# The last gate's last 128 weight rows in three transfers on GpSimd's queue, ahead of everything else there

## The chip, the cores and the metric

One core of one Trainium2 chip runs the whole program. The metric is the time of one execution in microseconds on the device; lower is better. All inputs begin in HBM, and the output goes back there.

## The reference

One decode step of a transformer block for four sequences, with six modulation vectors from a conditioning vector `c`. All is fp32.

```
mod = silu(c) @ w_mod          # [4, 6*512]: sa, ca, ga, sb, cb, gb
h = layernorm(x) * (1 + ca) + sa
x = x + ga * attention(h)      # 32 query heads, 8 kv heads, the last 2048 positions
h = layernorm(x) * (1 + cb) + sb
x = x + gb * ((silu(h @ w1) * (h @ w3)) @ w2)     # 512 -> 1792 -> 512
```

The change concerns `gb`, the gate of the last line: gb = silu(c) @ (columns 2560 to 3071 of `w_mod`), a sum over 512 weight rows of 512 columns. These rows are taken in four chunks of 128.

## The kernel before

The program is written without a scheduler: each engine's instructions are in source order, and semaphores tie the engines together. Almost all loads are issued on SP's queue by the helper `load` (L89), in the order in which they are used. Each load has 128 partitions, and its semaphore counts 16 when it has landed.

Two SBUF buffers of 16384 columns, `KV[0]` and `KV[1]`, take the keys and values of the eight kv heads in turn; a third one, `WP`, takes the query and output projection weights. First of all comes `T0` (L91), which lies in `KV[1]`: 16 columns of `c`, transposed, and the weights of `ca` and `sa`. ACT's queue loads the first query weights (L92) and `x` (L93). `KV[0]` follows on SP, and `KV[1]` once the product with `T0` is done (`pe` 1, L95).

At the start DVE and ACT take the first layer norm's statistics from `x`, then silu of the 16 columns (L182 to L188) gives `sc`, the stationary operand of all modulation products. DVE's `same` (L179) stands between them and waits for `ident`, which POOL makes. POOL begins with memsets and `ident` (L128 to L139); after that it only passes on load semaphores.

Attention runs in a loop of four pairs of heads on PE and ACT. After it come the modulation products of the middle (L381), the second layer norm, and the FFN: `w1` and part of `w3` from `KV[0]`, the rest of `w3` (`f2_in`) from `KV[1]`. All of the last loads go into `KV[1]` in this order: `f2_in` in two halves, `gb_in` (the four chunks of the gate's weights, 2048 columns), and `w2` in six blocks (`W2_CUTS`, semaphores `dw`). On PE the gate's four products (L454) go to four groups of partitions in one PSUM bank, `bM`; they are summed later by a product with `same` (L474), which is also the transposition that the output needs. The FFN's down projection takes the first eight blocks of 128 rows into `bO`, the last six straight into `bX`. Two DVE steps (L488, L490) and a store (L492) end the program.

Of the kernel before, what the change touches and what calls it, by code (L numbers as in the profile page):

```python
# [5 lines left out]
AF = mybir.ActivationFunctionType  # L6
# [4 lines left out]
B, D, HQ, G, SK, DH, W, FF = 4, 512, 32, 8, 8192, 128, 2048, 1792  # L11
P = 128
# [2 lines left out]
EPS = 1e-5  # L15
CHUNKS = [(j, c) for c in range(4) for j in range(4) if c < 2 or j < 3]
HEAD = 8
W2_CUTS = [0, 4, 8, 10, 12, 13, 14]
PAIRS = G // 2

# [20 lines left out]
        return (self.sem, self.n)  # L41


def block_kernel(nc, x_in, t0_in, t1_in, kv_in, w_in, wm_in, f1_in, f2_in, gb_in, w2_in, out):
    T, v, s, gp, S = nc.tensor, nc.vector, nc.scalar, nc.gpsimd, nc.sync

    def sems(names):
        return [nc.alloc_semaphore(n) for n in names.split()]

    def sb(name, cols, rows=P):  # L50
        return nc.alloc_sbuf_tensor(name, (rows, cols), F32).ap()

    def bank(name):
        return nc.alloc_psum_tensor(name, (P, 512), F32).ap()

    (first,) = sems("first")
    A = Queue(nc, s, "act")
    V = Queue(nc, v, "dve")
    L = Queue(nc, gp, "pool")
    dx, dt0, dt1, dkv, dk, dva, dvb, dwo, dm, df1, df2a, df2b, dgb = sems("dx dt0 dt1 dkv dk dva dvb dwo dm df1 df2a df2b dgb")  # L60
    dw = sems(" ".join(f"dw{i}" for i in range(len(W2_CUTS) - 1)))
    z_ok, q_ok, p_ok, k_ok, va_ok, vb_ok, pt_ok, o_ok, ot_ok = sems("z_ok q_ok p_ok k_ok va_ok vb_ok pt_ok o_ok ot_ok")
    s_done, q_done, qt_done, pp_done, o_done, x_done, a_done, pe, last = sems("s_done q_done qt_done pp_done o_done x_done a_done pe last")
    (nm_ok, lb_ok, dout) = sems("nm_ok lb_ok dout")

    KV = [sb("KV0", 16384), sb("KV1", 16384)]
    WP = sb("WP", 8192)
    T0 = KV[1][:, : 16 + 4096]
    x_sb = sb("x_sb", 512, B)
    ident, same, eps = sb("ident", P), sb("same", B), sb("eps", 1)  # L70
    sc, e1, e2 = sb("sc", 16), sb("e1", 16), sb("e2", 16)
    hT, h2T = sb("hT", 16), sb("h2T", 16)
    Z = sb("Z", B * 28)
    q_sb, p_sb, o_sb, a_sb, y_sb, g_sb, u_sb, gb_sb = [sb(n, 512) for n in "q_sb p_sb o_sb a_sb y_sb g_sb u_sb gb_sb".split()]
# [10 lines left out]
    bS, bQ, bT, bP, bO, bX, bA, bM = [bank(n) for n in "bS bQ bT bP bO bX bA bM".split()]  # L85


    def load(dst, src, sem):
        S.dma_start(dst, src).then_inc(sem, 16)  # L89

    load(T0, t0_in, dt0)  # L91
    s.dma_start(WP[:, 4096:], t1_in).then_inc(dt1, 16)  # L92
# [27 lines left out]
    S.wait_ge(x_done, G)  # L120
    load(KV[1][:, :3072], f2_in[:, :3072], df2a)
    load(KV[1][:, 3072:6144], f2_in[:, 3072:], df2b)
    load(KV[1][:, 6144:8192], gb_in, dgb)
    for a, b, sem in zip(W2_CUTS[:-1], W2_CUTS[1:], dw):
        load(KV[1][:, 8192 + a * 512 : 8192 + b * 512], w2_in[:, a * 512 : b * 512], sem)


    l_eps = L.op(gp.memset(eps, EPS))  # L128
    t = L.op(gp.memset(ident, 0.0))
    L.wait(t)  # L130
# [48 lines left out]
    v_same = V.op(v.tensor_reduce(same, ident.rearrange("p (j i) -> p i j", i=32)[:, :B, :], axis=AX.X, op=ALU.add))  # L179

    A.wait((dt0, 16))
    t = A.op(s.activation(e1, T0[:, :16], AF.Exp, scale=-1.0))  # L182
    V.wait(t)
    t = V.op(v.tensor_scalar(e2, e1, 1.0, None, op0=ALU.add))
    V.wait(t)
    t = V.op(v.reciprocal(e2, e2))
    V.wait(t, (dt0, 16))
    t_sc = V.op(v.tensor_mul(sc, T0[:, :16], e2))  # L188

    A.wait((pe, 1))  # L190
    t_sa = A.op(s.copy(sa_sb, bM[32 : 32 + B, :]))
# [1 line left out]
    t = V.op(v.scalar_tensor_tensor(xs, bM[:B, :], 1.0, xc, op0=ALU.add, op1=ALU.mult))  # L193
# [60 lines left out]
    def mm(o, lhsT, rhs, start=True, stop=True):  # L254
        return T.matmul(o, lhsT, rhs, start=start, stop=stop, skip_group_check=True)  # L255
# [46 lines left out]
    T.wait_ge(V.sem, t_sc[1])  # L302
    for k in range(4):
        for i in range(2):
            ins = mm(bM[32 * i : 32 * i + B, :], sc[:, k * B : (k + 1) * B], T0[:, 16 + (2 * k + i) * 512 : 16 + (2 * k + i + 1) * 512], k == 0, k == 3)
    ins.then_inc(pe, 1)
    T.wait_ge(V.sem, t_h[1])
    for k in range(4):
        ins = T.transpose(bT[:, k * B : (k + 1) * B], h[:, k * P : (k + 1) * P], ident[:B, :B])
# [71 lines left out]
    for k in range(4):  # L381
        for i in range(3):
            at = (3 * k + i) * 512
            ins = mm(bX[32 * i : 32 * i + B, :], sc[:, k * B : (k + 1) * B], KV[0][:, at : at + 512], k == 0, k == 3)
# [5 lines left out]
    t = V.op(v.tensor_mul(ag, bM[:B, :], ga_sb))  # L390
# [13 lines left out]
    for k in range(4):  # L404
        ins = T.transpose(bT[:, k * B : (k + 1) * B], h[:, k * P : (k + 1) * P], ident[:B, :B])
# [4 lines left out]
    def view(t_):  # L410
        return t_.rearrange("p (c j i) -> p c j i", c=4, j=4)
# [4 lines left out]
    for k in range(4):  # L416
        for j in range(4):
            at = 6144 + k * 2048 + j * 512
            ins = mm(bQ[32 * j : 32 * j + B, :], h2T[:, k * B : (k + 1) * B], KV[0][:, at : at + 512], k == 0, k == 3)
# [3 lines left out]
    for k in range(4):  # L423
# [5 lines left out]
        for j in range(3):  # L429
            at = k * 1536 + j * 512  # L430
            ins = mm(bA[32 * j : 32 * j + B, :], h2T[:, k * B : (k + 1) * B], KV[1][:, at : at + 512], k == 0, k == 3)
    ins.then_inc(pe, 1)
    A.wait((pe, 7))
    t = A.op(s.activation(view(eT), view(bP)[:, :, :, :B], AF.Exp, scale=-1.0))
    V.wait(t)
    t = V.op(v.tensor_scalar(dT, eT, 1.0, None, op0=ALU.add))
    V.wait(t)
    t = V.op(v.reciprocal(rT, dT))
# [7 lines left out]
    for c in range(4):  # L446
        ins = T.transpose(bS[:, c * P : c * P + 96], u_sb[:96, c * P : (c + 1) * P], ident[:96, :96])
# [3 lines left out]


    T.wait_ge(dgb, 16)
    for k in range(4):  # L454
        ins = mm(bM[32 * k : 32 * k + B, :], sc[:, k * B : (k + 1) * B], KV[1][:, 6144 + 512 * k : 6144 + 512 * (k + 1)])
    ins.then_inc(pe, 1)
    A.wait((pe, 10))
    t_gb = A.op(s.copy(gb_sb, bM))
    T.wait_ge(V.sem, t_hid[1])
    hw = view(hidT)  # L460
    w2 = KV[1][:, 8192 : 8192 + 14 * 512].rearrange("p (n m) -> p n m", n=14)
    for i in range(len(W2_CUTS) - 1):
        T.wait_ge(dw[i], 16)
        for n in range(W2_CUTS[i], W2_CUTS[i + 1]):
            jj, c = CHUNKS[n]
            if n < HEAD:
                ins = mm(bO[32 * (n % 4) : 32 * (n % 4) + B, :], hw[:, c, jj, :], w2[:, n, :], n < 4, n >= HEAD - 4)
                continue
            for j in range(4):
                ins = mm(bX[32 * j : 32 * j + B, :P], hw[:, c, jj, :], w2[:, n, j * P : (j + 1) * P], n == HEAD, n == 13)  # L470
        if i == 0:
            T.wait_ge(A.sem, t_gb[1])
            for j in range(4):
                ins = mm(bT[32 * j : 32 * j + B, :P], same, gb_sb[:, j * P : (j + 1) * P])  # L474
# [13 lines left out]
    t = V.op(v.tensor_mul(yt, bX[:, :P], gbJ))  # L488
# [8 lines left out]
def _layout(i):  # L497
    import numpy as np

    def a(t):  # L500
        return np.ascontiguousarray(t)

    k = i["A_k_cache"][:, :, SK - W :, :].reshape(B, G, NT, 512, DH)
    v = i["A_v_cache"][:, :, SK - W :, :].reshape(B, G, NT, 4, P, DH)
    k = k.transpose(1, 4, 2, 0, 3).reshape(G, P, 8192)
    v = v.transpose(1, 4, 2, 0, 3, 5).reshape(G, P, 8192)
    wm = i["w_mod"].reshape(4, P, 6, 512).transpose(1, 0, 2, 3)
    c = i["c"].reshape(B, 4, P).transpose(2, 1, 0).reshape(P, 16)
    wq = i["A_wq"].reshape(4, P, G, 512).transpose(2, 1, 0, 3).reshape(G, P, 2048)
    wo = i["A_wo"].reshape(G, R, P, D).transpose(0, 2, 1, 3).reshape(G, P, 2048)  # L510
    pairs = [[wo[2 * p], wo[2 * p + 1]] + ([wq[2 * p + 2], wq[2 * p + 3]] if p < 3 else [wo[6], wo[7]]) for p in range(4)]
    w1 = i["B_w1"].reshape(4, P, FF).transpose(1, 0, 2)
    w3 = i["B_w3"].reshape(4, P, FF).transpose(1, 0, 2)
    w2 = i["B_w2"].reshape(14, P, D)
    return {
        "x_in": a(i["A_x"].reshape(B, D)),
        "t0_in": np.concatenate([c, wm[:, :, 1::-1].reshape(P, 4096)], 1),
        "t1_in": np.concatenate([wq[0], wq[1]], 1),
        "kv_in": np.concatenate([k, v], 2),
        "w_in": np.stack([np.concatenate(p, 1) for p in pairs]),  # L520
        "wm_in": a(wm[:, :, 2:5]).reshape(P, 6144),
        "f1_in": np.concatenate([w1, w3[:, :, 1536:]], 2).reshape(P, 8192),
        "f2_in": a(w3[:, :, :1536]).reshape(P, 6144),
        "gb_in": a(wm[:, :, 5]).reshape(P, 2048),
        "w2_in": a(np.stack([w2[4 * j + c_] for j, c_ in CHUNKS], 1)).reshape(P, 14 * D),
    }

# [14 lines left out]
```

## Time and profile before

| | us |
|---|---|
| median of 3 runs | 243.06 (243.06 to 243.09) |
| the profiled execution, its own time | 243.12 |
| its span, first to last instruction | 241.8 |
| PE busy in the span | 136.2 |
| ordinary load queue (q1), share of sixteen DMA engines | 95.6% |

The page gives the busy time of the engines and of the DMA queues over the whole span. The chain of work that ended last is followed back from the store: it tells which transfer or instruction held the end. The busy table by stretches tells, for any piece of the span, how full the engines and the sixteen DMA engines were: a DMA share of 1.00 means all sixteen at work, and one sixteenth is 0.06. The list of instructions in order of time gives for each group its start, its length and, in brackets, how long its engine had been idle before it and what released it.

### The profile page before, as it was taken

Reading aid. Unit: us, or ns where it says so; the run is one execution under the profiler, and the core shown is the slowest. Engines: PE = TensorE matmul, PEld = TensorE weight load, DVE = VectorE, ACT = ScalarE, POOL = GpSimd, SP = SyncE. Lnnn points to the kernel's source line nnn. Section 1 sums busy time; section 2 is a strip of 40 time slices with the busy share of each in tenths; the row PEclk is TensorE's granted clock in tenths of the full one; section 3 lists DMA queues with packets and bytes.
Section 4 is the critical chain, followed back from the end, with each engine's and each line's share of the span. In section 5 each row is a group of like instructions: output and inputs, shape, how many; then the busy total and the mean of one; then the engine's idle time right before and its main releaser. Section 6 shows DMA issues by size and latency. Waiting matters only on the chain. (4 is left out here: it accounts for less than half of the span.)

```text
span 241.8 us, 2271 instructions
## 1 busy us (share of the span) xinstructions
PE 136.2 (56%) x940; PEld 37.3 (15%) x940; DVE 38.6 (16%) x126; ACT 25.1 (10%) x54; POOL 1.7 (1%) x14
## 2 busy tenths in 40 slices
PE   3004677817660387276723772667237768665964
PEld 0000121201210012112200121112001222111211
DVE  3003202202200022022000220220002222124122
ACT  2002002100120002001100020001001201123110
POOL 2000000000000000000000000000000000000000
PEclk9999959967996579987985798879858997995999
DMA  7998989899989898999898989998989999999992
GB/s 266 451 500 369 499 371 488 379 417 445 493 379 488 369 499 381 407 428 510 369 499 369 499 369 423 434 510 369 499 350 442 442 400 440 453 431 396 418 411 106
DMA packets 4044, 101.33 MB, mean 419 GB/s; under 512 B 452, under 2 KB 580, under 8 KB 1096
## 3 DMA queue, kind: packets, MB, share of 16 engines
q1 hardware_dynamic: 3888, 99.17, 95.6%
q10 hardware_dynamic: 152, 2.11, 2.1%
q8 instruction: 3, 0.05, 0.1%
q14 instruction: 1, 0.01, 0.0%
HBM read 101.20 MB, written 0.07 MB: 419 GB/s over the span
## 5 line engine op out<-in xcount | busy, mean ns | idle before, releaser
L255 PE MATMUL bS<-KV,Z 128*16 128x512 f32 x256 | 42.5, 824 | 38.8 <-PEq L258 38.8
L255 PE MATMUL bO<-KV,pT 128*16 128x512 f32 x256 | 31.9, 642 | 0.5
L255 PEld LDWEIGHTS bS<-KV,Z 128*16 128x16 f32 x256 | 9.1, 122 | 66.6 <-issue 66.6
L218 DVE TENSOR_REDUCE MX<-bS 128x1 f32<-128x512 f32 x8 | 5.5, 691 | 79.6 <-PE bS L255 79.6
L255 PE MATMUL bM<-KV,sc 128*4 128x512 f32 x24 | 7.3, 835 | 16.6 <-DVE sc L188 16.6
L367 ACT ACTIVATE p_sb<-bS,NB 128x512 f32<-128x512 f32 x8 | 5.5, 687 | 101.2 <-ACTq L358 101.2
L276 PE MATMUL bP<-ident,p_sb 128*128 128x128 f32 x32 | 5.0, 280 | 17.3 <-PEq L258 17.3
L255 PE MATMUL bA<-WP,oT 128*4 128x512 f32 x64 | 10.4, 728 | 5.2 <-PEq L258 5.2
L255 PEld LDWEIGHTS bO<-KV,pT 128*16 128x16 f32 x256 | 8.1, 105 | 22.9 <-issue 22.9
L372 ACT ACTIVATE o_sb<-bO,LB 128x512 f32<-128x512 f32 x8 | 5.5, 687 | 48.7 <-ACTq L358 48.7
L255 PE MATMUL bQ<-WP,hT 128*4 128x512 f32 x64 | 9.2, 648 | 0.6 <-DVE hT L197 0.6
L276 PE MATMUL bX<-ident,o_sb 128*128 128x128 f32 x32 | 5.0, 280 | 7.9 <-PEq L258 7.9
L244 DVE TENSOR_REDUCE oT<-bX 128x16 f32<-128x64 f32 x8 | 1.8, 224 | 44.0 <-PE bX L276 44.0
L276 PE MATMUL bT<-ident,q_sb 128*128 128x128 f32 x32 | 5.5, 298 | 3.6 <-PEq L258 3.6
L276 PEld LDWEIGHTS bP<-ident,p_sb 128*128 128x128 f32 x32 | 3.4, 140 | 24.4 <-issue 24.4
L276 PEld LDWEIGHTS bX<-ident,o_sb 128*128 128x128 f32 x32 | 3.4, 141 | 15.0 <-issue 15.0
L227 DVE COPY pT<-bP 128x256 f32<-128x256 f32 x8 | 3.4, 424 | 13.7 <-PE bP L276 13.7
L255 PE MATMUL bQ<-KV,h2T 128*4 128x512 f32 x32 | 5.3, 831 | 0.3 <-DVE h2T L408 0.3
L276 PEld LDWEIGHTS bT<-ident,q_sb 128*128 128x128 f32 x32 | 3.7, 150 | 8.3 <-issue 8.0
L255 PEld LDWEIGHTS bM<-KV,sc 128*4 128x4 f32 x24 | 1.0, 106 | 22.6 <-DVE sc L188 18.2
L255 PE MATMUL bX<-KV,sc 128*4 128x512 f32 x24 | 4.4, 592 | 0.0
L202 DVE TENSOR_REDUCE Z<-bT 128x16 f32<-128x64 f32 x8 | 1.8, 224 | 15.4 <-PE bT L276 15.1
(101 smaller groups left out, 68.0 us busy)
## 6 DMA issues: line engine op xcount, KB each, us to landing
WP<-w_in SPq DMA_DIRECT2D x3, 4096.0 KB, 18.9
KV<-kv_in SPq DMA_DIRECT2D x1, 4096.0 KB, 24.1
KV<-f_in SPq DMA_DIRECT2D x1, 4096.0 KB, 25.9
KV<-kv_in SPq DMA_DIRECT2D x1, 3072.0 KB, 30.9
KV<-wm_in SPq DMA_DIRECT2D x1, 3072.0 KB, 16.5
KV<-f_in SPq DMA_DIRECT2D x2, 1536.0 KB, 17.2
KV<-t_in SPq DMA_DIRECT2D x1, 2056.0 KB, 12.3
WP<-t_in ACTq DMA_DIRECT2D x1, 2048.0 KB, 12.5
```

What stands on the lines that cost most here:

```text
L202: v.tensor_reduce(Z.rearrange("p (b i) -> p b i", b=B)[:, :, 12 : 12 + R], bT.rearrange("p (r k i) -> p i r k", r=R, k=4)[:, :B], axis=AX. ...
L218: t = V.op(v.reduce_max(MX[:, 0:1], bS, axis=AX.X))
L227: v.tensor_copy(pT.rearrange("p (t b c r) -> p c b t r", t=NT, b=B, c=4), bP.rearrange("p (c b i) -> p c b i", c=4, b=B)[:, :, :, :16].rea ...
L244: V.op(v.tensor_reduce(oT.rearrange("p (r b) -> p r b", r=R), diag, axis=AX.X, op=ALU.add), ot_ok)
L255: return T.matmul(o, lhsT, rhs, start=start, stop=stop, skip_group_check=True)
L276: ins = T.transpose(dst[:, c * P : (c + 1) * P], src[:, c * P : (c + 1) * P], ident)
L367: A.op(s.activation(p_sb, bS, AF.Exp, bias=NB[:, 0:1], accum_out=SM[:, 0:1]), p_ok)
L372: A.op(s.mul(o_sb, bO, LB[:, 0:1]), o_ok)
```

## The change

The gate's last chunk, rows 384 to 511 of `w_mod`, leaves `gb_in` (now three chunks, 1536 columns) and comes in a new input `gc_in`. Its 128 rows are filled up with zeros to 132 and cut in three blocks of 44 rows, which lie beside each other in 1536 columns of a new tile `GC` with 80 partitions. The 44 rows of a block stand on partitions 0-11, 16-31 and 64-79. POOL fills `GC` with zeros and then issues three transfers, one for each band of partitions, with 3, 4 and 4 groups of four rows on the source's side. The source array has five rows to a group, of which four are read. Two very small transfers into a tile `GZ` that nothing reads stand between and behind them: one element, and four rows of two.

`T0` grows by 12 columns: the elements of `c` for the 44 partitions, three blocks by four sequences, zeros elsewhere; silu is taken of 28 columns instead of 16. On PE the gate's product has three chunks as before and three products over 80 partitions that are summed in the fourth group of `bM`. They wait for all five transfers (`dgc` at 80). The blocks of `w2` move down by 512 columns in `KV[1]`.

```
+    t = L.op(gp.memset(GC, 0.0))
+    L.wait(t)
+    at = 0
+    for row, e in BANDS:
+        gp.dma_start(GC[row : row + 4 * e], gc_in[at : at + e, :4]).then_inc(dgc, 16)
+        at += e
+        if e == 3:
+            gp.dma_start(GZ[:1, 2:3], gc_in[0, :1, :1]).then_inc(dgc, 16)
+    gp.dma_start(GZ[:, :2], gc_in[0, :4, :2]).then_inc(dgc, 16)
     l_eps = L.op(gp.memset(eps, EPS))
...
-    load(KV[1][:, 6144:8192], gb_in, dgb)
+    load(KV[1][:, 6144:7680], gb_in, dgb)
     for a, b, sem in zip(W2_CUTS[:-1], W2_CUTS[1:], dw):
-        load(KV[1][:, 8192 + a * 512 : 8192 + b * 512], w2_in[:, a * 512 : b * 512], sem)
+        load(KV[1][:, W2_AT + a * 512 : W2_AT + b * 512], w2_in[:, a * 512 : b * 512], sem)
...
-    t_sc = V.op(v.tensor_mul(sc, T0[:, :16], e2))
+    t_sc = V.op(v.tensor_mul(sc, T0[:, :C_IN], e2))
...
     T.wait_ge(dgb, 16)
-    for k in range(4):
-        ins = mm(bM[32 * k : 32 * k + B, :], sc[:, k * B : (k + 1) * B], KV[1][:, 6144 + 512 * k : 6144 + 512 * (k + 1)])
+    T.wait_ge(dgc, 80)
+    for k in range(3):
+        mm(bM[32 * k : 32 * k + B, :], sc[:, k * B : (k + 1) * B], KV[1][:, 6144 + 512 * k : 6144 + 512 * (k + 1)])
+    for m in range(SUB):
+        ins = mm(bM[96 : 96 + B, :], sc[:80, 16 + m * B : 16 + (m + 1) * B], GC[:, m * 512 : (m + 1) * 512], m == 0, m == SUB - 1)
...
+SUB = 3
+BANDS = [(0, 3), (16, 4), (64, 4)]
+C_IN = 16 + 4 * SUB
+W2_AT = 6144 + 1536
```

On POOL, at the start of the program, this stands in a row before:

```order
L128 MEMSET eps 128x1 [waits barrier_Pool_Activation_PE_DVE_SP_gather]
L129 MEMSET ident 128x128
L132 ISA [waits pool]
L132 AFFINE_SELECT ident<-ident 128x128
L135 MEMSET y_sb 128x512
```

and now:

```order
L134 MEMSET GC 80x1536 [waits barrier_Pool_Activation_PE_DVE_SP_gather]
L138 DMA GC<-gc_in 12x1x1536 [waits pool]
L141 DMA GZ<-gc_in 1x1
L138 DMA GC<-gc_in 16x1x1536 x2
L142 DMA GZ<-gc_in 4x2
L143 MEMSET eps 128x1
L144 MEMSET ident 128x128
L147 ISA [waits pool]
L147 AFFINE_SELECT ident<-ident 128x128
```

A memset and five issues have moved in ahead of `eps` and `ident`.

On PE, at the last gate between the FFN's transposition (`bS`) and the down projection (`bO`), this stands before:

```order
L447 MATMUL bS<-ident,u_sb 128x96 x3
L255 MATMUL bM<-KV,sc 4x512 [waits dgb]
L255 MATMUL bM<-KV,sc 4x512 x3
L255 MATMUL bO<-KV,hidT 4x512 [waits dw0,dve]
L255 MATMUL bO<-KV,hidT 4x512 x3
L255 MATMUL bT<-gb_sb,same 4x128 [waits act]
```

and now:

```order
L462 MATMUL bS<-ident,u_sb 128x96 x3
L270 MATMUL bM<-KV,sc 4x512 [waits dgc,dgb]
L270 MATMUL bM<-KV,sc 4x512 x2
L270 MATMUL bM<-GC,sc 4x512 x3
L270 MATMUL bO<-KV,hidT 4x512 [waits dw0,dve]
L270 MATMUL bO<-KV,hidT 4x512 x3
L270 MATMUL bT<-gb_sb,same 4x128 [waits act]
```

Six matmuls stand where four stood, and the first of them waits for one semaphore more; the down projection and the product with `same` follow behind them as before.

## Rows read from the trace of the kernel before

**Rows 1.** The page: span, DMA queues (packets, MB, share); and the chain's end.
```profile
span 241.8 us, 2271 instructions
...
q1 hardware_dynamic: 3888, 99.17, 95.6%
...
q8 instruction: 3, 0.05, 0.1%
q14 instruction: 1, 0.01, 0.0%
...
212.29 26.78 DMA KV<-w_in
...
239.11 0.45 PE bX L255 x8
```

**Rows 2.** Busy table by stretches, from 180 us to 238.64.
```profile
core 0: us, PE busy (x) PEld busy (x) DVE busy (x) ACT busy (x) POOL busy (x), PEclk, DMA share, GB/s
...
180.00:236.00 56.00, 41.16 (x298) 10.76 (x290) 12.67 (x39) 9.19 (x22) 0.00 (x0) 0.88 1.00 425
236.00:236.90 0.90, 0.65 (x16) 0.28 (x16) 0.47 (x1) 0.00 (x0) 0.00 (x0) 1.00 1.00 373
236.90:237.36 0.46, 0.46 (x22) 0.16 (x12) 0.22 (x1) 0.00 (x0) 0.00 (x0) 1.00 0.46 151
237.36:237.95 0.59, 0.30 (x12) 0.09 (x8) 0.00 (x0) 0.00 (x0) 0.00 (x0) 1.00 0.19 73
237.95:238.64 0.69, 0.69 (x24) 0.35 (x23) 0.00 (x0) 0.00 (x0) 0.00 (x0) 1.00 0.12 48
```

**Rows 3.** Instruction packets in 34:37, 94:97, 213:216 and 236.9:238.7, queue, packets, MB, share.
```profile
q8 instruction: 1, 0.02, 2.1%
...
q14 instruction: 1, 0.01, 0.7%
...
q8 instruction: 1, 0.02, 2.3%
...
q8 instruction: 1, 0.02, 3.8%
```

**Rows 4.** Instructions in order of time from the last gate; then one tile's lengths (ns).
```profile
231.86 1.04 PE L255 MATMUL bM<-KV,sc 128*4 128x512 f32 x8
232.90 1.04 PE L255 MATMUL bO<-KV,hidT 128*4 128x512 f32 x8
232.97 0.58 ACT L458 COPY gb_sb<-bM 128x512 f32<-128x512 f32 x1 [3.95 <-PE bM L255]
233.75 0.40 PE L255 MATMUL bT<-gb_sb,same 128*4 128x128 f32 x8
235.32 1.04 PE L255 MATMUL bO<-KV,hidT 128*4 128x512 f32 x8 [1.16 <-DMA KV<-w_in]
236.43 0.69 DVE L481 COPY y_sb<-bO 128x512 f32<-128x512 f32 x1 [4.26 <-PE bO L255]
...
L255 PE MATMUL bM<-KV,sc x8: 592/592/593, 231.9 to 232.3; 128*4 128x512 f32 x8
```

**Rows 5.** Instructions in order of time at the program's start and at SP's third load.
```profile
1.43 0.52 POOL L135 MEMSET y_sb<- 128x512 f32 x1
2.27 0.20 POOL L139 MEMSET x1J<- 128x128 f32 x1
17.85 0.67 DVE L175 TENSOR_REDUCE st<-x_sb 4x1 f32<-4x512 f32 x1 [14.82 <-DMA x_sb<-x_in]
20.46 0.16 DVE L179 TENSOR_REDUCE same<-ident 128x4 f32<-128x16 f32 x1
27.57 0.33 SPq L89 DMA_DIRECT2D KV<-kv_in  x1
```

**Rows 6.** DMA issues: name, queue, count, KB each, us to landing.
```profile
KV<-t_in SPq DMA_DIRECT2D x1, 2056.0 KB, 12.3
WP<-t_in ACTq DMA_DIRECT2D x1, 2048.0 KB, 12.5
```

More of the change, by code (lines that the diff above doesn't have):

```diff
@@ L17 @@
 HEAD = 8
+SUB = 3
+BANDS = [(0, 3), (16, 4), (64, 4)]
+ROWS = [p for at, e in BANDS for p in range(at, at + 4 * e)]
+C_IN = 16 + 4 * SUB
+W2_AT = 6144 + 1536
 W2_CUTS = [0, 4, 8, 10, 12, 13, 14]
@@ L41, in op, with block_kernel @@
         return (self.sem, self.n)
-def block_kernel(nc, x_in, t0_in, t1_in, kv_in, w_in, wm_in, f1_in, f2_in, gb_in, w2_in, out):
+def block_kernel(nc, x_in, t0_in, t1_in, kv_in, w_in, wm_in, f1_in, f2_in, gb_in, gc_in, w2_in, out):
     T, v, s, gp, S = nc.tensor, nc.vector, nc.scalar, nc.gpsimd, nc.sync
@@ L59, in block_kernel @@
     L = Queue(nc, gp, "pool")
-    dx, dt0, dt1, dkv, dk, dva, dvb, dwo, dm, df1, df2a, df2b, dgb = sems("dx dt0 dt1 dkv dk dva dvb dwo dm df1 df2a df2b dgb")
+    dx, dt0, dt1, dkv, dk, dva, dvb, dwo, dm, df1, df2a, df2b, dgb, dgc = sems("dx dt0 dt1 dkv dk dva dvb dwo dm df1 df2a df2b dgb dgc")
     dw = sems(" ".join(f"dw{i}" for i in range(len(W2_CUTS) - 1)))
@@ L67, in block_kernel @@
     WP = sb("WP", 8192)
-    T0 = KV[1][:, : 16 + 4096]
+    GC, GZ = sb("GC", SUB * 512, 80), sb("GZ", 4, 4)
+    T0 = KV[1][:, : C_IN + 4096]
     x_sb = sb("x_sb", 512, B)
     ident, same, eps = sb("ident", P), sb("same", B), sb("eps", 1)
-    sc, e1, e2 = sb("sc", 16), sb("e1", 16), sb("e2", 16)
+    sc, e1, e2 = sb("sc", C_IN), sb("e1", C_IN), sb("e2", C_IN)
     hT, h2T = sb("hT", 16), sb("h2T", 16)
@@ L181, in block_kernel @@
     A.wait((dt0, 16))
-    t = A.op(s.activation(e1, T0[:, :16], AF.Exp, scale=-1.0))
+    t = A.op(s.activation(e1, T0[:, :C_IN], AF.Exp, scale=-1.0))
     V.wait(t)
@@ L304, in block_kernel @@
         for i in range(2):
-            ins = mm(bM[32 * i : 32 * i + B, :], sc[:, k * B : (k + 1) * B], T0[:, 16 + (2 * k + i) * 512 : 16 + (2 * k + i + 1) * 512], k == 0, k == 3)
+            ins = mm(bM[32 * i : 32 * i + B, :], sc[:, k * B : (k + 1) * B], T0[:, C_IN + (2 * k + i) * 512 : C_IN + (2 * k + i + 1) * 512], k == 0, k == 3)
     ins.then_inc(pe, 1)
@@ L460, in block_kernel @@
     hw = view(hidT)
-    w2 = KV[1][:, 8192 : 8192 + 14 * 512].rearrange("p (n m) -> p n m", n=14)
+    w2 = KV[1][:, W2_AT : W2_AT + 14 * 512].rearrange("p (n m) -> p n m", n=14)
     for i in range(len(W2_CUTS) - 1):
@@ L508, in _layout @@
     c = i["c"].reshape(B, 4, P).transpose(2, 1, 0).reshape(P, 16)
+    last = np.zeros((SUB * len(ROWS), B + 512), c.dtype)
+    last[:P, :B] = i["c"].reshape(B, 512)[:, 384:].T
+    last[:P, B:] = i["w_mod"][384:, 5 * 512 :]
+    last = last.reshape(SUB, len(ROWS), B + 512).transpose(1, 0, 2)
+    cs = np.zeros((P, SUB * B), c.dtype)
+    gc = np.zeros((len(ROWS) // 4, 5, SUB * 512), c.dtype)
+    gc[:, :4] = last[:, :, B:].reshape(len(ROWS) // 4, 4, SUB * 512)
+    cs[ROWS] = last[:, :, :B].reshape(len(ROWS), SUB * B)
     wq = i["A_wq"].reshape(4, P, G, 512).transpose(2, 1, 0, 3).reshape(G, P, 2048)
@@ L516, in _layout @@
         "x_in": a(i["A_x"].reshape(B, D)),
-        "t0_in": np.concatenate([c, wm[:, :, 1::-1].reshape(P, 4096)], 1),
+        "t0_in": np.concatenate([c, cs, wm[:, :, 1::-1].reshape(P, 4096)], 1),
         "t1_in": np.concatenate([wq[0], wq[1]], 1),
@@ L523, in _layout @@
         "f2_in": a(w3[:, :, :1536]).reshape(P, 6144),
-        "gb_in": a(wm[:, :, 5]).reshape(P, 2048),
+        "gb_in": a(wm[:, :3, 5]).reshape(P, 1536),
+        "gc_in": gc,
         "w2_in": a(np.stack([w2[4 * j + c_] for j, c_ in CHUNKS], 1)).reshape(P, 14 * D),
```

## The prediction

> **What bounds the kernel now.** I read the page first: of a span of 241.8 us the ordinary DMA queue fills 95.6% of what sixteen DMA engines have, and the chain that ended last is at its end one transfer, the last block of the second FFN weight, issued at 212.29 us and landing 26.78 us later, at 239.07 [rows 1]. After it come eight short matmuls at 239.11, two DVE steps and the store. So time is won only where the last bytes land earlier.
>
> Then the busy table by stretches. From 180 to 236 us the DMA share is 1.00, and still 1.00 up to 236.90. Then it falls in steps: 0.46, then 0.19 up to 237.95, which is three sixteenths, then 0.12 up to 238.64, which is two sixteenths [rows 2]. That is the thing to see: the load is level until about 237, thirteen engines are done by 237.36, one works on to 237.95 and two to 238.64. Everything waits for those two, because a transfer's semaphore is full only when the last engine has delivered. 238.64 plus 0.43 to the landing is 239.07.
>
> Why are three behind? Every load covers 128 partitions, so each engine has the same bytes. What is not equal is the instruction traffic: one 16 KB packet near 34 to 37 us, one of 8 KB near 94 to 97, one of 16 KB near 213 to 216, and one of 16 KB after 236.9 [rows 3]. Three of these fall while the queue is full, in sizes 2 : 1 : 2. The ends at 238.64, 237.95 and 238.64, against about 237.3 for the others, are 1.3, 0.65 and 1.3 us late, again 2 : 1 : 2. I read that as three different engines, each of which carried one of them and, since the queue never ran dry, never caught up. The fourth came when most engines were done.
>
> [...]
>
> **The change, part by part.**
>
> The gate load shrinks from 2048 to 1536 columns of fp32: 2048 bytes less per partition, eight partitions per engine, 16,384 bytes. From 180 to 236 us sixteen engines at share 1.00 moved 425 GB/s, 26.6 GB/s each [rows 2]. That takes 0.617 us off every engine. With the smaller packets of 236.00 to 236.90 (373 GB/s, 23.3 each) it would be 0.70; I take 0.617, since the gate's rows of 6 to 8 KB are nearer to the long stretch.
>
> The first load grows by 12 columns, 48 bytes a partition, 384 bytes an engine: plus 0.014 us for all.
>
> The three new transfers bring 44 partitions of 6144 bytes. Each engine that carries four of them gets 24,576 bytes, 0.925 us at the same rate. [...] Eleven engines then have 0.925 - 0.617 + 0.014 = 0.32 us more than before, and five have 0.60 us less. No view of the trace names a DMA engine, so which five is not to be read there. That is the open term, and it has two answers. If both last engines are among the five, they end at 238.64 - 0.60 = 238.04, and the eleven by 237.36 + 0.32 = 237.68, which is earlier; the end moves by **0.60 us**. If one of the two is among the eleven, the end moves to 238.96, 0.32 later. I take the first, and it is a choice. What the trace gives for it is a shape: queue 14's packet of 8 KB went to one engine, queue 8's three packets of 16 KB to three others [rows 3], since the two last ends are two engines, both late by one packet only, and the third packet added nothing to either. [...] Against it: were the late engines drawn blindly from sixteen, both last ones would be among the five once in twelve.
>
> [...]
>
> **POOL's start.** A memset of 80 x 1536 and five issues now stand ahead of everything else on POOL. A 512-column memset takes 0.52 us [rows 5], so the new one about 1.6. The trace has no issue from POOL; the nearest rows are SP's, 0.33 us [rows 5]. Bounds: nothing visible, and some 2 us each, six times SP's; so POOL's last memset, begun at 2.27 us, moves to between 3.9 and 13.9. Behind it wait PE's first dummy matmul and DVE's `same` at 20.46, which itself stands behind the arrival of x at 17.85 [rows 5]. That cover is 18 us; cost nothing. x lies behind the first loads and rides on few engines; the added 0.92 us on some of them can bring x, the modulation matmuls and the second KV load's issue (27.57) that much later. Ahead of that load lie 2056 + 2048 KB [rows 6] and 8.39 MB of KV: 12.6 MB, which at 425 GB/s take 29.6 us even if counted from the span's start. 27.57 + 0.33 + 0.92 is 28.8, so the queue does not run dry and this costs nothing either.
>
> **The gate's matmuls.** Before, four matmuls to four column groups run together: 231.86 to 232.90 [rows 4]. Now three and one run together and two more follow in the fourth group. The round's entries (two for each fp32 matmul) last 0.59 us each and start between 231.9 and 232.3 [rows 4], so a round is 1.04 - 0.59 = 0.45 us of starts; two more are 0.9 us. The new wait on the five transfers is met some 220 us earlier. Queued behind on PE is the first block of the last weight (232.90), then the gate's turn, held by ACT's copy at 232.97; both move 0.9 us later, to about 233.8 and 234.7. The next block's landing now releases PE at 235.32, and by the shift at 234.72: PE is ready for it near 235.1, some 0.4 us late. The y copy (236.43) then comes at about 236.2, and the last block lands at 238.47, so over 1 us of room is left ahead of the final eight matmuls. Cost nothing. If the cover were gone the 0.4 us would stand in the sum.
>
> **Sum.** Against the profiled execution's own 243.12 us (span 241.8 and 1.3 around it): 243.12 - 0.60 = 242.52. The runs' median of 243.06 is 0.06 lower and gives 242.46. Forecast: **242.5 us**, about 0.25% faster.
>
> **Rivals.**
>
> *A last engine among the eleven.* [...] For it: nothing in the trace names an engine. Against: only the shape told above. Time 243.12 + 0.32 = 243.44, slower by 0.13%.
>
> *All sixteen carry them.* The blocks are then not confined: one row to each of sixteen engines for the two 16-row blocks, and one more on twelve. A last engine gets 12,288 bytes, 0.46 us: -0.60 + 0.46 = -0.14, so 242.98, no change; with a third row it is +0.09, 243.21. [...] The change would then not do what it says.
>
> *The last fetch moves.* The 16 KB packet after 236.9 came as the engines ran out. PE now executes some nine instructions more before it, and everything at the end is 0.60 us earlier, so it can meet an engine that still has blocks to carry. By the late ends that costs that engine up to 1.3 us. On an unloaded engine, done near 237.3 - 0.6 = 236.7, it ends by 238.0, just no loss; on one of the eleven, 237.6 + 1.3 = 238.9 at worst, a loss of the whole gain: 242.5 to 243.4, about 243.0.
>
> *POOL holds the start.* The mechanism is the wait of DVE's `same` on POOL's `ident`, ahead of the conditioning vector on DVE. It decides once POOL is later than 20.46 us by what is left at the second KV load, 29.6 - 27.9 = 1.7 us, so from 22.2 us on: five issues of over 3.6 us each, eleven times SP's. At 5 us each POOL ends at 2.47 + 1.6 + 25 = 29.1, and the queue stands dry for up to 29.1 - 22.2 = 6.9 us: 243.12 - 0.60 + 6.9 = 249.4 at most, slower. Against it: the 0.33 us of the nearest row [rows 5].
>
> **How the numbers follow.** Forecast 0.70, all sixteen 0.08, a last engine among the eleven 0.11, the last fetch 0.08, POOL 0.03. The likeliest gives 242.5; its own range, by the 0.617 to 0.70 us and by a few tenths of reserve at the tail, is 242.3 to 242.8. To hold 8 in 10 the range goes on to the spread case and most of the fetch case, to 243.2; what is left out is the loaded last engine and POOL. About 0.2%, 0.49 us, is what a measurement of this kernel can tell from no change. The forecast is beyond that by only 0.1 us, so of its 0.70 some 0.11 go to no change: faster 0.59, same 0.36, slower 0.05.
>
> **What the profile after would show.** Right: the tail of the busy table has its step of two sixteenths end near 238.0, and the last landing stands near 238.47; the gate's matmuls take about 1.9 us in place of 1.04 without any later PE wait growing; the first KV loads have no gap. Wrong: two sixteenths still busy at 238.9 (a loaded last engine), or at 238.5 (spread over all); an instruction packet that lies in the last full stretch with its own late end; a hole in the DMA row near 30 us, with DVE's `same` waiting for POOL. The forecast falls with the choice of the five: if a last engine carries a block, nothing else here makes up for it.

## The result, and the profile after

The changed kernel is slower. Six runs gave a median of 244.08 us (243.15 to 245.22) against 243.07 us (243.00 to 243.16) before on the same chip; the ratio is 1.0045 with an interval of 1.0027 to 1.0062. Forecast was 242.5, with 243.2 as the far end. The profiled execution took 243.79 us.

The page of the changed kernel, first the span, then the queues (packets, MB, share of sixteen engines' time):

```profile
span 242.5 us, 2286 instructions
...
q1 hardware_dynamic: 3888, 98.91, 95.5%
...
q0 software_dynamic: 304, 0.27, 0.3%
```

Beside [rows 1] this holds the main reading. 98.91 + 0.27 MB are the 99.17 MB of before to within rounding, so the bytes are the same. Their packets took 95.8% of 242.5 us, 232.3 us of each engine's time on average, where 95.6% of 241.8 us, 231.2, were enough before. That is some 1.1 us more (plus or minus 0.2 by the rounding of the shares) on the average engine, for bytes that only moved. The forecast had no such term: its eleven engines' +0.32 and five engines' -0.60 are +0.03 on average.

The queues by stretches tell where most of it lies. First from 17 to 44 us, where 0.20 of the 0.27 MB for `GC` move and the ordinary queue has KV rows of 64 KB, before and after; then from 44 to 236 us, before and after:

```profile
q1 hardware_dynamic: 204, 12.32, 105.4%
```
```profile
q1 hardware_dynamic: 191, 11.47, 101.1%
q0 software_dynamic: 191, 0.20, 2.1%
```
```profile
q1 hardware_dynamic: 3119, 81.98, 99.3%
```
```profile
q1 hardware_dynamic: 2985, 82.23, 99.6%
```

At the rate of before, 11.47 MB would take 98.1% of the 27 us; they took 3.0% of 27 us more, 0.80 us of the average engine's time. After 44 us the rows take the same time per byte as before, 1.21% of the stretch for each MB in both. (A packet counts whole where it starts, so a share can go over 100%.)

The busy table at the end, the stretches of [rows 2] and one more (the last two columns are DMA share and GB/s):

```profile
236.00:236.90 0.90, 0.90 (x7) 0.15 (x9) 0.00 (x0) 0.58 (x1) 0.00 (x0) 1.00 1.00 394
236.90:237.36 0.46, 0.46 (x13) 0.26 (x16) 0.00 (x0) 0.06 (x1) 0.00 (x0) 1.00 1.04 396
237.36:237.95 0.59, 0.59 (x12) 0.15 (x8) 0.00 (x0) 0.20 (x1) 0.00 (x0) 1.00 1.01 365
237.95:238.64 0.69, 0.58 (x20) 0.28 (x12) 0.48 (x1) 0.00 (x0) 0.00 (x0) 1.00 0.46 175
238.64:239.01 0.37, 0.11 (x4) 0.11 (x8) 0.21 (x1) 0.00 (x0) 0.00 (x0) 1.00 0.12 44
```

Before, the engines were full to 236.90 and two of them worked on alone for the better part of a microsecond, to 238.64. Now all are full to 237.95 and two end at 239.01. So the tail behind the bulk did become shorter, but the bulk ends about a microsecond later, and the end moved from 238.64 to 239.01: +0.37 where -0.60 was expected.

And the end no longer hangs on the load. The last pieces of the chain of waits (start, length, what):

```profile
233.47 1.40 PE bM L270 x9
234.88 0.41 PE bM L270
235.31 0.84 PE bM L270 x2
236.15 0.86 PE bO L270 x2
237.01 0.22 PE bT L270 x8
237.23 0.90 PE bO L270 x8
238.13 0.02 issue
238.16 0.70 DVE y_sb L499
238.86 0.04 issue
238.90 1.32 PE bX L270 x40
240.22 0.02 issue
240.24 0.30 DVE yt L506
```

In [rows 1] a transfer stands there, and eight matmuls at 239.11. Now the chain holds no transfer: it runs from the gate's products on PE through `bO` and DVE's `y_sb` copy to forty entries into `bX`. The reason is in the order of time around the gate, beside [rows 4]:

```profile
233.40 0.60 PE L270 MATMUL bM<-KV,sc 128*4 128x512 f32 x3
...
233.42 0.59 PE L270 MATMUL bM<-GC,sc 80*4 80x512 f32 x1
...
234.28 0.60 PE L270 MATMUL bO<-KV,hidT 128*4 128x512 f32 x3
234.70 0.59 PE L270 MATMUL bM<-GC,sc 80*4 80x512 f32 x1
...
234.71 0.60 PE L270 MATMUL bO<-KV,hidT 128*4 128x512 f32 x3
235.13 1.02 PE L270 MATMUL bM<-GC,sc 80*4 80x512 f32 x2
...
235.99 1.02 PE L270 MATMUL bO<-KV,hidT 128*4 128x512 f32 x2
...
236.19 0.58 ACT L476 COPY gb_sb<-bM 128x512 f32<-128x512 f32 x1 [5.64 <-PE bM L270]
```

The three products with `GC` are six passes, two for each, all into the fourth group of partitions, and they start 0.43 us apart: the first at 233.42, the last near 235.56 (not all rows are shown). Six entries of `bO`, for the other three groups, run in between; the two left over come behind at 235.99. The gate's copy on ACT begins at 236.19, against 232.97 before.

At the start, POOL's rows lie inside the forecast's bounds (start, length, engine, what):

```profile
0.74 1.38 POOL L134 MEMSET GC<- 80x1536 f32 x1 [0.29 <-POOLq L562]
...
2.42 0.70 POOL L138 DMA_DIRECT2D GC<-gc_in  x1 [0.31 <-POOL GC L134]
...
3.63 1.15 POOL L138 DMA_DIRECT2D GC<-gc_in  x2
...
6.86 0.20 POOL L154 MEMSET x1J<- 128x128 f32 x1
...
18.80 0.67 DVE L190 TENSOR_REDUCE st<-x_sb 4x1 f32<-4x512 f32 x1 [15.77 <-DMA x_sb<-x_in]
```

POOL is through near 7.1 us, and `x` comes 0.95 us later than in [rows 5], 18.80 for 17.85, where 0.92 had been allowed.

### The profile page after: what moved, and what is told of

It reads as the page before. It is cut to its first block, busy times and chain, and to the rows that moved or that the text cites. A ratio compares the mean times of both kernels' runs of the same rounds, so it can differ in the third digit from the quotient of the medians.

```text
span 242.5 us, 2286 instructions
## 1 busy us (share of the span) xinstructions
PE 136.5 (56%) x944; PEld 38.6 (16%) x944; DVE 38.7 (16%) x126; ACT 25.1 (10%) x54; POOL 6.0 (2%) x20
## 3 DMA queue, kind: packets, MB, share of 16 engines
q1 hardware_dynamic: 3888, 98.91, 95.5%
## 5 line engine op out<-in xcount | busy, mean ns | idle before, releaser
L270 PE MATMUL bS<-KV,Z 128*16 128x512 f32 x256 | 44.3, 855 | 41.2 <-PEq L273 41.2
L291 PE MATMUL bP<-ident,p_sb 128*128 128x128 f32 x32 | 5.5, 298 | 17.3 <-PEq L273 17.3
L270 PE MATMUL bM<-KV,sc 128*4 128x512 f32 x22 | 5.9, 722 | 13.1 <-DVE sc L203 13.1
L270 PEld LDWEIGHTS bO<-KV,pT 128*16 128x16 f32 x256 | 8.2, 104 | 22.3 <-issue 22.3
L270 PE MATMUL bQ<-WP,hT 128*4 128x512 f32 x64 | 8.3, 592 | 0.6 <-DVE hT L212 0.6
L270 PE MATMUL bA<-y_sb 128*128 128x512 f32 x2 | 2.1, 1142 | 7.1 <-POOL x1J L154 7.1
L217 DVE TENSOR_REDUCE Z<-bT 128x16 f32<-128x64 f32 x8 | 1.8, 225 | 14.5 <-PE bT L291 14.2
## 6 DMA issues: line engine op xcount, KB each, us to landing
KV<-f_in SPq DMA_DIRECT2D x2, 1536.0 KB, 16.8
```

Source lines behind the costliest of these rows:

```text
L217: v.tensor_reduce(Z.rearrange("p (b i) -> p b i", b=B)[:, :, 12 : 12 + R], bT.rearrange("p (r k i) -> p i r k", r=R, k=4)[:, :B], axis=AX. ...
L291: ins = T.transpose(dst[:, c * P : (c + 1) * P], src[:, c * P : (c + 1) * P], ident)
```

## The experiments

Two questions: where the microsecond on every engine comes from, and what the tail on PE costs beside it.

**The five issues without their bytes.** Before, with the memset and the five transfers, each row one element; the gate is as before.

```
+    for row, e in BANDS:
+        gp.dma_start(GC[row : row + 4 * e], gc_in[at : at + e, :4]).then_inc(dgc, 16)   # rows of 4 bytes
...
+    T.wait_ge(dgc, 80)
```

> The kernel before, with the changed kernel's five GpSimd transfers at the same place and with the same rows, but one fp32 element to a row (the gate's load and products stay as before; nothing reads the new tile). Theory 1, the GpSimd transfers cost every DMA engine the same whatever they carry: the changed kernel's last two engines ended at 239.01 us where 238.04 was worked out, so some 0.95 us on each engine; the last landing goes from 239.07 to about 240.0 and the time from 243.1 to about 244.0. Theory 2, the 24 KB per engine on a late engine are the cause: without the bytes nothing changes, 243.1.

Measured 243.22 us (243.05 to 244.41), ratio 1.0015 (1.0004 to 1.0026). The issues cost a little, about a sixth of the loss by the medians. The rest needs the bytes.

**The long gate without the load.** Before, with the fourth gate product made three times in the same group.

```
-    for k in range(4):
+    for k in (0, 1, 2, 3, 3, 3):
```

> The kernel before, with its loads as they were, but the gate's fourth product made three times over into the same place (same values each time), so that PE runs three products one after another in the fourth column group as in the changed kernel. Theory 3, the serial products make PE late at the end: the gate's products last about 2.7 us in place of 1.04, the y copy begins near 237.0 in place of 236.43, and since the last blocks land only at 239.07 the time moves by 0 to 0.2 us, 243.1 to 243.3. Rival, the serial products alone explain the slower kernel: 244.

Measured 243.01, ratio 1.0003 (0.9994 to 1.0011). The serial passes alone cost nothing: the gate's products took 2.69 us (232.26 to 234.95) for 1.04, in a stage that began 0.4 us later than before, and the time is the same.

**The three products ahead of the tail.** The changed kernel, with the `GC` products behind the middle modulation products, some 20 us earlier.

```
+    T.wait_ge(dgc, 80)
+    for m in range(SUB):
+        mm(bM[96 : 96 + B, :], sc[:80, 16 + m * B : 16 + (m + 1) * B], GC[:, m * 512 : (m + 1) * 512], m == 0, m == SUB - 1)
     A.wait((pe, 4))
```

> The changed kernel with the three products over the new tile moved ahead, behind the middle's modulation products, where PE waits 5 us for the layer norm; the last gate has three products. Theory 1: the DMA end stays where it was, near 239.0 with the landing at 239.45, so 243.4 to 243.6, and what the changed kernel lost beyond that came from PE. Theory 3 as the only cause: back to 242.5.

Measured 243.67 (243.46 to 244.50), ratio 1.0037 (1.0023 to 1.0051). The chain ends with the last transfer again, the last eight matmuls wait for it until

```profile
239.61 0.45 PE bX L270 x8
```

which was 239.11 before. By the medians the load's side is worth about 0.6 us of the 1.0 and the tail on PE the other 0.4. By the two profiled executions it is 0.5 and 0.2: the first step behind the last matmuls, `yt`, begins at 239.57 before, at 240.08 here and at 240.24 in the changed kernel. The load is the larger part by both; the intervals of the two ratios overlap, so the exact split is not shown. All further kernels keep the early products, and what they show is the load.

**Another queue.** 44 neighbouring partitions (0 to 43) in one transfer, nothing on GpSimd: first on ACT's queue behind `x`, then on SP's between `T0` and `KV[0]`.

```
     s.dma_start(x_sb, x_in).then_inc(dx, 16)
+    s.dma_start(GC, gc_in).then_inc(dgc, 16)      # the second kernel: load(GC, gc_in, dgc)
     load(KV[0], kv_in[0], dkv)
```

> As the run with the early products, but the 132 rows lie on 44 neighbouring partitions and come in one transfer on ACT's queue behind x; no GpSimd transfer is left. Theory 1: without the GpSimd transfers the 0.60 us come back: the last engines end near 238.0 if they carry none of it, 242.5; if the engine that ended at 237.95 carries 24 KB it ends near 238.3 and the time is 242.8. Theory 2, the last engines are among those that carry it: end near 239.0, 243.4.

> As the run with 44 neighbouring partitions on ACT's queue, but the one transfer stands on SP's queue, between the first load and KV[0], so that no second queue runs beside the 64 KB rows of KV[0]. Theory M, small rows of a second queue beside the 64 KB rows slow the rows of all sixteen engines: the cost is gone, the last engines end 0.60 us earlier or, if the third late engine carries rows, at 237.95 + 0.32; landing near 238.7, time 242.7 to 242.8. Theory S, the cost comes from eleven engines falling out of step with five: it stays, 243.5 to 243.9.

Measured 243.92, ratio 1.0042 (1.0029 to 1.0055), and 244.08, ratio 1.0038 (1.0024 to 1.0051). A loss of that size needs no GpSimd queue, and no second queue beside SP's.

**All 128 partitions.** The same two places in the kernel before, with the chunk uncut: 128 partitions of 2048 bytes, one early product, the first load 16 columns wide as before.

```
+    GC = sb("GC", 512)
+    s.dma_start(GC, gc_in).then_inc(dgc, 16)      # the second kernel: load(GC, gc_in, dgc)
```

> The gate's last 128 rows as they are, 128 partitions of 2048 bytes, equal on all sixteen engines, early on ACT's queue behind x; one product over 128 partitions, made early; nothing else differs from the kernel before. Theory M: the second queue's rows slow all engines, 243.5 to 244.0, with fewer GB/s between 12 and 44 us than the 453 of the kernel before. Theory S: all engines stay in step, 243.1.

> The same 128 partitions of 2048 bytes on SP's queue between the first load and KV[0]. The control: bytes only moved, all engines equal, one queue. Both theories 243.1, the two last engines ending near 238.64 as before; if it is slower than 243.3, moving the bytes early costs something by itself.

Measured 243.01, ratio 1.0000 (0.9991 to 1.0009), and 243.11, ratio 1.0002 (0.9993 to 1.0011). Loading early, and 512 columns fewer in the last loads, costs and brings nothing. The loss lies in what the kernels with 44 partitions do differently, their 12 further columns in the first load among it.

**First on ACT's queue.** The 44 partitions ahead of the query weights and `x`.

```
+    s.dma_start(GC, gc_in).then_inc(dgc, 16)
     s.dma_start(WP[:, 4096:], t1_in).then_inc(dt1, 16)
```

> 44 neighbouring partitions on ACT's queue, but as its first transfer, so that the rows run beside the first load's 16 KB rows and are through before KV[0]. Theory M, if it needs the 64 KB rows: 242.7 to 242.9. Theory S, or M with any rows: 243.5 to 243.9.

Measured 251.40, ratio 1.0343 (1.0329 to 1.0357): a loss of another kind. Order of time, then a piece of the busy table:

```profile
29.60 0.67 DVE L181 TENSOR_REDUCE st<-x_sb 4x1 f32<-4x512 f32 x1 [26.58 <-DMA x_sb<-x_in]
...
39.11 0.33 SPq L94 DMA_DIRECT2D KV<-kv_in  x1
```
```profile
34.00:38.00 4.00, 4.00 (x12) 0.60 (x10) 0.00 (x0) 0.00 (x0) 0.00 (x0) 1.00 0.00 0
```

`x` arrives at 29.60, so the product with `T0` and the second KV load come at 39.11 instead of 27.57 [rows 5], and from 34 to 38 us the DMA share is 0.00. That is the dry queue of the rival on POOL's start, by way of `x`.

**48 and 88 partitions.** On SP's queue: 48 partitions of 6144 bytes in place of 44; and the 264 KB of the 44 as 88 partitions of 3072 bytes, 88 rows of the chunk whole and the last 44 (four of them zeros) as left and right halves, with one early product of 512 columns and two of 256.

```
-NR = 44
+NR = 48
```
```
-    GC = sb("GC", SUB * 512, NR)      # NR = 44
+    GC = sb("GC", 768, NR)            # NR = 88
```

> The run with 44 neighbouring partitions on SP's queue (median 244.08, ratio 1.0038) with one number changed: 48 partitions in place of 44, the blocks filled up with zeros to 3 x 48 rows. [...]

> [...] Theory T (wider first load): 243.6 to 244.1.

Measured 244.29, ratio 1.0053 (1.0039 to 1.0067), and 243.79, ratio 1.0038 (1.0024 to 1.0051). Both lose, so the loss is not bound to 44 rows. How the rows are shared among the engines is not shown, since no view here names an engine or a partition. Theory T is still open.

**The first load's 12 columns.** Added to the 128-partition load, taken from the 48-partition one.

> The run with 128 partitions of 2048 bytes on SP's queue (243.11, ratio 1.0002) with the first load widened by 12 columns of zeros, as the changed kernel has it; silu of 28 columns; nothing else. [...] Theory R (the rows of 3072 or 6144 bytes of a load that covers only a part of the partitions, while the long KV rows begin): as without the 12 columns, 243.1, ratio 1.000 to 1.001.

> The run with 48 partitions of 6144 bytes on SP's queue (244.29, ratio 1.0053) with the first load back at 16 columns; the three early products of the gate's last chunk take a stationary operand that is already there, so this chunk's contribution to the gate is not the reference's; the work is the same. Theory T (wider first load): the loss is gone, 243.0 to 243.2, ratio 1.000. Theory R (the load's rows themselves): as before the edit, 244.1 to 244.4, ratio 1.004 to 1.006.

Measured 243.06, ratio 1.0001 (0.9992 to 1.0010), and 244.42, ratio 1.0054 (1.0040 to 1.0068). The 128 partitions lose nothing with the 12 columns, and the 48 lose without them: Theory T falls.

**Row length, cover, place.** 128 partitions of 3072 bytes; 48 partitions in three loads of 2048-byte rows; 64 partitions of 4096 bytes; and the 44 partitions in the middle of attention.

```
+        if p == 1:
+            load(GC, gc_in, dgc)
         S.wait_ge(x_done, 2 * p + 1)
```

> The run with 128 partitions of 2048 bytes on SP's queue (243.11) with rows of 3072 bytes, the last 256 columns zeros that nothing reads. Each engine gets 24,576 bytes in place of 16,384, +0.31 us at 26.6 GB/s. Theory L (rows longer than 2048 bytes are slow there): 0.31 and a loss of 0.5 to 0.9 more, 243.9 to 244.3, ratio 1.0035 to 1.005. Theory C (the load covers only a part of the partitions): 0.31 alone, 243.3 to 243.5, ratio 1.001 to 1.0015.

> The run with 48 partitions of 6144 bytes on SP's queue (244.29, 244.42 with the narrow first load) with the same bytes to the same places in three loads of 48 rows of 2048 bytes. Theory L (row length): the loss is gone, 243.1 to 243.3, ratio 1.000 to 1.001. Theory C (part of the partitions): it stays, 244.0 to 244.5, ratio 1.004 to 1.006.

> [...] Theory L (row length over 2048): a loss as with the other long rows, 243.7 to 244.4, ratio 1.003 to 1.005. Theory C (part of the partitions): the loss shrinks with the cover, from 48 partitions' 1.3 us to between 0.3 and 1.0 with 64 partitions, 243.4 to 244.1. [...]

> The run with 44 neighbouring partitions on SP's queue (244.08) with that load moved from the start to the middle of attention, behind the second pair's projection weights and ahead of KV rows. Theory C or L, in any place: the loss stays, 243.6 to 244.1. Theory B (only beside the first KV rows, at the program's start): bytes alone count, eleven engines +0.32 and five -0.60, so 242.4 to 242.6 if the engines that end last are among the five, 243.3 to 243.5 if not.

Measured 243.39 (1.0017, 1.0008 to 1.0025), 244.44 (1.0057, 1.0044 to 1.0070), 243.89 (1.0041, 1.0028 to 1.0054) and 244.16 (1.0052, 1.0035 to 1.0070). That settles length and place: the longer rows on 128 partitions cost their bytes, 48 partitions lose with short rows as well, and the middle of attention is no better than the start. Whether fewer rows than 128 are enough for the loss is left to the next pair. The queue's row over 100 to 140 us (packets, MB, share), before and with the load there:

```profile
q1 hardware_dynamic: 356, 17.37, 100.4%
```
```profile
q1 hardware_dynamic: 407, 17.38, 102.7%
```

The same bytes take 2.3% of 40 us more, 0.9 us on the average engine.

**The same 64 rows, spread.** On every second partition of 128; and the 88 rows moved up to partitions 40 to 127.

```
+    S.wait_ge(L.sem, 1)
-    load(GC, gc_in, dgc)
+    load(GC[::2], gc_in, dgc)
```

> The run with 64 partitions of 4096 bytes on SP's queue (243.89, ratio 1.0041) with the same 64 rows on every second partition of a tile of 128, the others filled with zeros by POOL first; the load waits for that memset, and the early products run over 128 partitions with zeros in the stationary operand. [...] Theory D (rows crowd on a part of the partitions, or on those of other engines): the loss is gone, 243.0 to 243.3, ratio 1.000 to 1.001. Theory F (fewer than 128 rows, wherever they land): it stays, 243.7 to 244.1, ratio 1.003 to 1.005.

> The run with 88 partitions of 3072 bytes on SP's queue (243.79, ratio 1.0038) with the rows on partitions 40 to 127 in place of 0 to 87; partitions 0 to 39 are filled with zeros by POOL, and the early products run over 128 partitions. [...] Theory F (fewer than 128 rows): the same within 0.2 us, 243.6 to 244.0.

Measured 243.02, ratio 0.9998 (0.9989 to 1.0007), and 244.17, ratio 1.0048 (1.0034 to 1.0062). The first makes the cleanest pair of the study. The queue from 11.5 to 17 us, 64 rows on partitions 0 to 63, then on every second one:

```profile
q1 hardware_dynamic: 128, 2.36, 114.5%
```
```profile
q1 hardware_dynamic: 128, 2.36, 99.8%
```

The same 128 packets of the same 2.36 MB took 14.7% of 5.5 us more, 0.81 us of the average engine's time; the times differ by 0.87. Beside the partitions only a memset on POOL, the load's wait for it and rows of zeros in the early products differ, and these are additions in the faster kernel. Theory F falls, D stands. D has two halves, rows that crowd on a part of the partitions and rows that land on those of other engines; this pair does not tell them apart. The 88 rows moved up lost 0.4 more than at 0 to 87, where theory F allowed 0.2, and the intervals overlap; I take that as undecided.

The other kernels on SP's queue in the same stretch:

```profile
q1 hardware_dynamic: 192, 2.49, 105.9%
```
```profile
q1 hardware_dynamic: 112, 2.39, 123.4%
```
```profile
q1 hardware_dynamic: 148, 2.38, 117.4%
```
```profile
q1 hardware_dynamic: 146, 2.30, 120.6%
```
```profile
q1 hardware_dynamic: 103, 2.37, 114.4%
```

These are 128 partitions of 3072 bytes, 48 partitions, 88 at 0 to 87, 88 at 40 to 127, and 44. At the spread kernel's 99.8% for 2.36 MB their bytes would take 105.3, 101.1, 100.6, 97.3 and 100.2%. So the first loses 0.03 us, next to nothing, and the others 22.3, 16.8, 23.3 and 14.2% of 5.5 us: 1.2, 0.9, 1.3 and 0.8 us. What sets the size of the loss is not shown.

## Why the prediction was wrong

**The step that failed** is the cost of the three transfers: 24,576 bytes at 26.6 GB/s, +0.925 us on eleven engines and nothing on the other five. That eleven engines carry them, four rows each, was assumed, and no run shows it. The sum priced the rows by their own bytes alone. What the trace shows in its place is a price on the KV rows that are in flight beside them: 0.80 us of the average engine's time between 17 and 44 us, and none after. In the sum the end should move by -0.60 and moved by +0.37; the missing 0.97 us agrees with the 1.1 (plus or minus 0.2) by which the page's queue time grew. Of that the 0.80 us are the larger part; the empty issues cost 0.15 us by the medians.

Why the KV rows become slower in the changed kernel stays open. Shown is that its loss comes mostly with the bytes and not with the issues, that it lies on the KV rows beside them, and that it is of the size which other loads of 44 rows have on SP's and ACT's queue; for 64 rows the pair above shows that the partitions make it. Not shown is that the partitions make it in the changed kernel too, since my kernels with 44 partitions changed the queue and the partitions together: they lie on 0 to 43, the changed kernel's bands on 0-11, 16-31 and 64-79. The changed kernel with its bands on other partitions would tell; that was not tried. Open as well is why the changed kernel's six times spread over 2.1 us, where those of before spread over 0.2; a trace is of one execution.

**The late engines.** In the profile after, the two last engines end 1.1 us behind the bulk (239.01 against 237.95), where it was 1.7 before (238.64 against 236.90). That fits the 0.6 us of the choice of the five, but no view names an engine, so the choice itself is not shown. Whatever was gained was lost in a bulk that ends a microsecond later. The sign given for a loaded last engine, two sixteenths busy at 238.9, did come, and by itself it would have misled: with a bulk that ends 1.05 us late (237.95 for 236.90), unloaded last engines come out near 239.1 (238.04 and 1.05) and loaded ones near 240.0 (238.96 and 1.05). The rivals with a loaded last engine (243.44) and with all sixteen (242.98) were nearer in time, but by luck: neither has the bulk late.

**The gate's matmuls** were mis-sized. Two rounds more at 0.45 us were to make 1.9 us of 1.04; measured are 2.75, from 233.40 to 236.15. Each of the three products with `GC` had two passes, and the six in the one group started 0.43 us apart, one behind the other: two more products are four more passes, 1.7 us. The step took 0.45 us, the distance between the two passes of a product, for the whole product.

**"Over 1 us of room"** was true of before, and the tripled product confirms it: 1.65 us more of gate (2.69 for 1.04), no loss. It did not hold for the changed kernel. There attention's end is late already, and with it the issue of the last loads on SP and all of the FFN. SP's own row, before and after:

```profile
208.59 0.80 SPq L89 DMA_DIRECT2D KV<-f_in  x2
```
```profile
209.97 0.80 SPq L95 DMA_DIRECT2D KV<-f_in  x2
```

The gate begins at 233.40 for 231.86 [rows 4], and `y_sb` is copied at 238.16 instead of the forecast's 236.2. By the medians the tail is then worth the 0.4 us between 243.67 and 244.08, by the profiled executions 0.2. The forecast let the load's end and PE's work move independently; both hang on the same queue.

**Right:** POOL's start (its last memset begins at 6.86 us, inside 3.9 to 13.9; with the five issues it cost at most the 0.15 us of the kernel without bytes), `x` later by 0.95, no dry queue, and no new late engine by an instruction packet: at the end two sixteenths are busy, as before (0.12). What the traces and times show beside it: 128 partitions cost nothing beyond their bytes in four kernels (ratios 1.0000 to 1.0002, and 1.0017 with 3072 bytes), neighbouring rows on a part of them 0.8 us or more in nine (ratios 1.0038 to 1.0057). The 64 spread rows show that it need not be 128 rows.

## What to carry to other kernels

Where the DMA engines are the bound, as here with 95.6% of their time in one queue, look beside a transfer's own bytes at what its rows do to the loads beside them, and at the partitions on which they land. If a tile must be smaller than 128 rows, try its rows spread over all partitions (64 rows on every second partition were free, on the first 64 they cost 0.8 us on the average engine). Relieving an engine that ends last is worth at most what is taken off it, here 0.6 us, and a price like the 0.8 us on the average engine here eats it at once. The matmul products that are summed in one column group ran one pass after another here, 0.43 us each; make such products early, or in separate groups, before counting on the cover of a stage that other changes may move.

## What the runs showed that I had not expected

A load of neighbouring rows on a part of the partitions cost far more than its bytes among 64 KB rows: 0.8 to 1.3 us on the average of sixteen engines for about a quarter of a megabyte, at the start or in the middle, with rows of 2 to 6 KB, and a loss of that size came from either hardware queue. Five tiny transfers from GpSimd, with the memset ahead of them, cost about 0.15% (0.04 to 0.26%). And with a transfer put first on ACT's queue the small one behind it, `x`, came 11.7 us later, enough to let the queue run dry and cost some 8.4 us.
